# Conversion steps and their additions spread anew over the first slots of a threshold-attention kernel, and pair 0's q turned in two PSUM tiles

## The chip, the cores and the metric

The kernel runs on one core of a Trainium2 chip. The metric is the time of one launch on the device in microseconds (us). Engines are named as the profile names them: PE is TensorE's matmul stream and PEld its weight loads, DVE is VectorE, ACT is ScalarE, POOL is GpSimd, SP is SyncE, which here only issues DMAs. "L208" is line 208 of the kernel as it was before the change.

## The reference

Two blocks follow each other. The first is attention with a threshold, over 8 batches of 8 heads, 576 rows and 64 columns per head:

```python
scores = scale * np.matmul(q, k.transpose(0, 1, 3, 2))
thresh = np.max(scores, axis=-1, keepdims=True) - tau
scores = np.where(scores >= thresh, scores, -1000000000.0)
scores = scores - np.max(scores, axis=-1, keepdims=True)
attn = np.exp(scores)
attn = attn / (np.sum(attn, axis=-1, keepdims=True) + 1e-09)
return np.matmul(attn, v).astype(np.float32)
```

The second takes the result as x, 4608 rows of 512, through two layers with an exact GELU between them:

```python
h = x @ w_in
inv_sqrt2 = np.float32(1.0 / np.sqrt(2.0))
g = 0.5 * h * (1.0 + erf(h * inv_sqrt2))
return (g @ w_out).astype(np.float32)
```

`w_in` is 512 x 2048 and `w_out` 2048 x 512. Both weight arrays reach the kernel as float64, 8 bytes an element, while the kernel computes in float32. It therefore converts them on the chip.

## The kernel before, in words

**Pairs, chunks and slots.** Two heads make a pair; the 64 columns of the two heads fill the 128 partitions. The 576 rows of a pair are four chunks of 128 rows and a tail of 64. The tails of both heads share one chunk (number 4), so a pair has five chunks, and the main loop (L1169 to L1291) runs over slots, each one chunk of one pair. In chunks 0 to 3 a slot has two heads and so two score tiles, two maxima, two exponentials. Chunk 4 has one of each: it is called a one-head slot here. The first batch, four pairs, is ordered apart: slots 0 to 7 are chunks 0 and 1 of pairs 0 to 3, slots 8 to 19 are chunks 2, 3 and 4 of pairs 0 to 3. So slots 10, 13, 16 and 19 have one head. From slot 20 on come the other batches.

**One slot.** `scores` (L432) has PE write the scores of the chunk into PSUM. `softmax_head` has DVE take the negated row maximum (`nmx`, L444), POOL make the threshold from it (`thr`, L447) and ACT the exponential (`p`, L449). `softmax_tail` (L465, DVE) zeroes what lies under the threshold and sums the rows. PE transposes `p` in the next slot (L373), ACT copies the transposes out (L383, L395), and PE multiplies with v (`weigh_v`, L635 and L603). Between these, PE is given matmuls of the second block (`fill`, L703 and others) as soon as there are rows and weights for them.

**The conversion.** The weights are cut in 32 pieces of 128 x 512. SP loads a raw piece (`load_piece`, L184). One step of the conversion is four instructions on three engines: ACT scales the high and the low words (`convert_first`, L200 and L201); DVE shifts and masks the exponent and mantissa (L208) and joins the sign (L209), in `convert_second`, which also loads the next piece; POOL adds the low bits (`add_low_bits`, L220), after which the piece can be used by PE. The list `STEPS` gives the number of steps at the end of each slot. Their additions are not issued with them but wait in a list, `sums_due`, for the next slot's `softmax_head`. There, right after the first maximum has been issued, one addition is put ahead of the threshold on POOL: the newest of the list. After the head, all others follow. The order of every engine's instructions is that in which the program issues them.

**The rest that shares these engines.** `DIVIDE_LATE` tells in which slot the rows of x of a pair are divided by their sums (`divide_late`, L509, two products on POOL). `divisors_early` (L485 to L497) makes those divisors, with DMAs on SP's queue. In slots with `long` set, some of the conversion's ACT work is issued early (`convert_ahead`).

**The start.** `turn_qk_early(0)` turns q and k of pair 0 by matmuls with the identity: `most("k")` turns k in one PSUM tile (L324, copied by DVE at L329), `tails` turns the last 64 rows of both (L336, L341; copies L344, L345, L348), and `most("q", 2)` turns q in two halves of one PSUM tile, each copied by ACT (L327). The tails of q and v are zeroed by DVE (L1128 and L1129), behind four small DVE instructions that need tau (L1118 to L1122).

Of the kernel before, what the change touches and what calls it, by code (L numbers as in the profile page):

```python
# [8 lines left out]
FP32 = mybir.dt.float32  # L9
# [9 lines left out]
def kernel(  # L19
# [28 lines left out]
    nc = tc.nc  # L48
    ctx.enter_context(tc.manual_schedule())

    B, H, S, D = q.shape
    d_model, d_ff = moe_w_in.shape
    P = 128
# [4 lines left out]
    NC = S // P  # L58
# [21 lines left out]
    ps = ctx.enter_context(tc.tile_pool(name="ps", bufs=4, space=PSUM))  # L80
# [21 lines left out]
    def x_slot(want=None):  # L102
        i = max(x_free) if want is None else want
        x_free.remove(i)
        return i
# [8 lines left out]
    def x_rows(i):  # L114
        return xall[:, i, :, :].rearrange("p c t -> p (c t)")
# [5 lines left out]
    ident = const.tile([P, P], FP32, name="ident")  # L121
# [3 lines left out]
    q_tail = [att.tile([P, P], FP32, name=f"q_tail{i}") for i in range(4)]  # L125
    v_sb = [att.tile([P, 2, KR, D], FP32, name=f"v{i}") for i in range(4)]
# [19 lines left out]
    for _ in range(3):  # L146
# [4 lines left out]
    pieces = [(w_in_sb[c][:, f:f + PIECE], moe_w_in[c * P:(c + 1) * P, f:f + PIECE])  # L151
              for f in range(0, d_ff, PIECE) for c in range(N_DM)]
# [60 lines left out]

    sums_due = []

    def add_low_bits(newest=False):

        for _ in range(min(1, len(sums_due)) if newest else len(sums_due)):
            dst, power = sums_due.pop(-1 if newest else 0)
            nc.gpsimd.tensor_tensor(dst, power, dst, op=ALU.add)  # L220
            converted[0] += 1

# [42 lines left out]
    def load_early(p):  # L265
        b, hp = divmod(p, HP)
        s = st[p] = {}
        for name, src in (("q", q), ("k", k)):

            if p == 2:  # L270
                at = s[name + "_slot"] = x_slot()
                t = x_rows(at)[:, 0:2 * (NC + 1) * D].rearrange("p (e c d) -> p e c d", e=2, d=D)
            else:
                t = ld.tile([P, 2, NC + 1, D], FP32, tag=name, name=name)
            s[name] = t
            eng = (nc.scalar, nc.gpsimd)[p] if p < 2 and name == "k" else nc.sync
            for e in range(2):
                rows = src[b, 2 * hp + e, 0:MAIN, :]
                if name == "q":
                    eng.dma_start(t[:, e, 0:NC, :].rearrange("p (g c) d -> p g (c d)", c=2),  # L280
                                  rows.rearrange("(g p c) d -> p g (c d)", p=P, c=2))
                else:
                    eng.dma_start(t[:, e, 0:NC, :], rows.rearrange("(p t) d -> p t d", p=P))
            eng.dma_start(t[0:TAIL, :, NC, :], src[b, 2 * hp:2 * hp + 2, MAIN:S, :].rearrange("e s d -> s e d"))
# [15 lines left out]
    def turn_qk_early(p, names="qk"):  # L300


        s = st[p]
        if names == "k":
            qT, kT = s["qT"], s["kT"]
        elif 2 <= p < HP:
            qT = op.tile([P, MAIN], FP32, tag="o_sb", name="qT")
            kT = pd_tail[p - 2].rearrange("p b i -> p (b i)")
        else:
            qT = ld.tile([P, MAIN], FP32, tag="qT", name="qT")  # L310
            kT = ld.tile([P, TAIL + S], FP32, tag="kT", name="kT")
        s["qT"], s["kT"] = qT, kT
        qt = s["q_tail"] = q_tail[p % 4]
        copy = nc.scalar.copy if p else nc.vector.tensor_copy
        tiles = {name: s.pop(name) for name in names}

        def most(name, parts=1):
            t = tiles[name]
            tr = ps.tile([P, NC, P], FP32, tag="mm", name="tr")
            n = NC // parts  # L320
            for part in range(parts):
                for c in range(part * n, (part + 1) * n):
                    for e in range(2):
                        nc.tensor.matmul(tr[e * D:(e + 1) * D, c, :], lhsT=t[:, e, c, :], rhs=ident, start=True, stop=True)  # L324
                src = tr[:, part * n:(part + 1) * n, :].rearrange("p c s -> p (c s)")
                if name == "q":
                    nc.scalar.activation(qT[:, part * n * P:(part + 1) * n * P], src, AF.Copy, bias=0.0, scale=q_scale)  # L327
                else:
                    copy(kT[:, TAIL:S], src)  # L329

        def tails():
            tr = ps.tile([P, NC, P], FP32, tag="mm", name="tr")
            if "q" in names:
                none = q_tail[HP - 1][0:TAIL, D:2 * D]
                for e in range(2):
                    nc.tensor.matmul(tr[e * D:(e + 1) * D, 0, (1 - e) * TAIL:(2 - e) * TAIL], lhsT=ident[0:TAIL, 0:D],  # L336
                                     rhs=none, start=True, stop=True)
            for j, name in enumerate(names):
                for e in range(2):
                    at = e * TAIL if name == "q" else 0  # L340
                    nc.tensor.matmul(tr[e * D:(e + 1) * D, j, at:at + TAIL], lhsT=tiles[name][0:TAIL, e, NC, :],  # L341
                                     rhs=ident[0:TAIL, 0:TAIL], start=True, stop=True)
            if "k" in names:
                nc.scalar.copy(kT[:, S:S + TAIL], tr[:, j, 0:TAIL])  # L344
                nc.scalar.copy(kT[D:P, 0:TAIL], tr[D:P, j, 0:TAIL])  # L345
            if "q" in names:
                yield
                nc.scalar.activation(qt, tr[:, 0, :], AF.Copy, bias=0.0, scale=q_scale)  # L348

        if p == 0:  # L350
            most("k")
            rest = tails()
            next(rest)
            most("q", 2)
            next(rest, None)
            return
        for name in names:
            most(name)
        for _ in tails():
            pass  # L360
        x_free.extend(s.pop(name + "_slot") for name in names if name + "_slot" in s)
# [73 lines left out]
    def softmax_head(p, i):  # L435

        s = st[p]
        n = len(s["sc", i])
        nmx = small.tile([P, 2], FP32, tag="nmx", name="nmx")
        thr = s["thr", i] = small.tile([P, 2], FP32, tag="thr", name="thr")  # L440
        w = s["p", i] = work.tile([P, 2 * S], FP32, tag="p", name="p")
        for e in range(n):
            sc = s["sc", i][e][:, :, 0:HALF]
            nc.vector.tensor_reduce(nmx[:, e:e + 1], sc, axis=AXIS.XY, op=ALU.max, negate=True)  # L444
            if e == 0:
                add_low_bits(True)
            nc.gpsimd.tensor_scalar(  # L447
                thr[:, e:e + 1], nmx[:, e:e + 1], -1.0, tau_eff, op0=ALU.mult, op1=ALU.subtract)
            nc.scalar.activation(  # L449
                w[:, e * S:(e + 1) * S].rearrange("p (h s) -> p h s", h=2), sc, AF.Exp, bias=nmx[:, e:e + 1], scale=1.0)  # L450
# [23 lines left out]
    def invert(p, i):  # L474

        den = st[p]["sum", i]
        nc.vector.reciprocal(den, den)
# [636 lines left out]
        assert not beside  # L1114

    load_early(0)
    some = const.tile([P, 1], FP32, name="some")
    nc.vector.tensor_scalar(some, tau_sb, 0.0, None, op0=ALU.is_ge)  # L1118
    nc.vector.tensor_scalar(q_scale, some, SCALE, None, op0=ALU.mult)
# [5 lines left out]
    load_early(2)  # L1125
    for _ in range(4):
        load_piece(nc.sync)
    for t in q_tail + [t[:, :, NC, :] for t in v_sb]:  # L1128
        nc.vector.memset(t, 0.0)  # L1129
    turn_qk_early(0)  # L1130
    load_v_early(0)
    load_early(3)
# [23 lines left out]

    PARTS = 1.3, 1.3, 0.2, 1.3, 0.9

    DIVIDE_LATE = {14: 0, 16: 1, 19: 2, 22: 3}
    STEPS = [0, 1, 1, 1, 1, 1, 1, 1, 1, 2, 2, 2, 3, 2, 2, 3, 3, 3, 1, 0, 1]  # L1160
    BUSY = {1: 2, 6: 2, 8: 2}

    tokens = 0
# [5 lines left out]
    for n in range(len(slots) + WEIGH + 1):  # L1169
        p, i = slots[n] if n < len(slots) else divmod(n, SLOTS)  # L1170
        early = p < EARLY
        last = slots[n - 1] if 0 < n <= len(slots) else None
        if p < NP:
            scores(p, i)
            softmax_head(p, i)
            add_low_bits()
            if last and last[0] < EARLY and last[1] < 2:
                invert(*last)
            if last and last[0] < EARLY and last[1] == NC:
                divisors_early(last[0])  # L1180
            if p == 0 and i == 0:
                turn_qk_early(1)
            elif p < HP - 1 and i < 2 and n > 1:
                turn_qk_early(p + 1, "qk"[i])
        elif n == len(slots):
            early_end.close()
            weights_first()
# [16 lines left out]
        if long:  # L1204
            convert_ahead(STEPS[n] - 1)
        if n in DIVIDE_LATE:
            divide_late(DIVIDE_LATE[n])
        if p > EARLY and i == WEIGH:
# [56 lines left out]
        elif n in (BATCH - 2, BATCH - 1):  # L1265
            turn_qk(HP, "k" if n == BATCH - 2 else "q")
        convert(STEPS[n] if n < len(STEPS) else 0)
        if not early:
# [58 lines left out]
```

## Time and profile before

| | us |
|---|---|
| runs | 1329.33, 1327.56, 1326.86 |
| their median | 1327.56 |
| the profiled execution | 1327.03 |
| its span, first to last instruction | 1325.3 |
| PE busy | 1313.4 (99%) |
| DVE busy | 1042.8 (79%) |
| ACT busy | 601.9 (45%) |
| POOL busy | 634.2 (48%) |

The span is part of the profiled execution; the 1.7 us around it belong to the launch. The busy shares are means over the whole span. Up to about slot 20 (120.75 us) all four engines are loaded, after it PE alone is nearly always busy. The first row maxima of the slots concerned are at 53.30 us (slot 9), 58.77 (10), 63.76 (11), 69.23 (12), 76.55 (13), 82.50 (14), 88.46 (15), 95.29 (16), 102.77 (17), 110.58 (18), 116.01 (19) and 120.75 (20).

The durations, in us, that matter for those slots, as the groups and the timeline of the profile have them: L208 0.42 where nothing disturbs it, L209 0.69, L444 0.75, L465 0.82, L447 0.29, L449 0.74, L200 and L201 0.70 each, L220 1.27, L509 0.74 and 0.32. Instructions that follow each other directly on DVE or ACT overlap by some 0.08 us in the records, so a step of L208 and L209 takes 1.07 and the second of two L465 adds 0.74.

### The profile page before, as it was taken

Reading aid. Unit: us, or ns where it says so; the run is one execution under the profiler, and the core shown is the slowest. Engines: PE = TensorE matmul, PEld = TensorE weight load, DVE = VectorE, ACT = ScalarE, POOL = GpSimd, SP = SyncE. Lnnn points to the kernel's source line nnn. Section 1 sums busy time; section 2 is a strip of 40 time slices with the busy share of each in tenths; the row PEclk is TensorE's granted clock in tenths of the full one; section 3 lists DMA queues with packets and bytes.
Section 4 is the critical chain, followed back from the end, with each engine's and each line's share of the span. In section 5 each row is a group of like instructions: output and inputs, shape, how many; then the busy total and the mean of one; then the engine's idle time right before and its main releaser. Section 6 shows DMA issues by size and latency. Waiting matters only on the chain.

```text
span 1325.3 us, 19980 instructions
## 1 busy us (share of the span) xinstructions
PE 1313.4 (99%) x6362; PEld 890.3 (67%) x6362; DVE 1042.8 (79%) x2009; ACT 601.9 (45%) x1018; POOL 634.2 (48%) x1058
## 2 busy tenths in 40 slices
PE   9999999999999999999999999999999999999998
PEld 7775476576476466466466466478778787877877
DVE  6888877888888888888888888883857698386674
ACT  7888266376376367357457438232111203211120
POOL 3565555465555555565555541236364403645430
PEclk9999999999999999999999999999999999999999
DMA  8453676767777777787787775400000140000003
GB/s 256 161 178 106 145 164 159 166 156 168 189 164 164 191 181 165 193 190 168 184 192 170 176 165 115 100 9 0 1 1 0 40 110 11 0 1 0 1 0 80
DMA packets 213688, 153.14 MB, mean 116 GB/s; under 512 B 117264, under 2 KB 196992, under 8 KB 213584
## 3 DMA queue, kind: packets, MB, share of 16 engines
q1 hardware_dynamic: 195440, 125.31, 40.4%
q0 software_dynamic: 17712, 26.26, 7.5%
q8 instruction: 52, 0.85, 0.3%
q14 instruction: 52, 0.43, 0.1%
q10 hardware_dynamic: 432, 0.30, 0.1%
HBM read 56.62 MB, written 12.58 MB: 52 GB/s over the span
## 4 chain that ended last, share of the span: by engine, by line
PE 93%; DVE 2%; issue 1%; DMA 1%; ACT 1%; POOL 1%; SPq 0%; POOLq 0%; DVEq 0%; ACTq 0%
PE bank L891 34%; PE o_ps L718 17%; PE hT L703 16%; PE sc L432 13%; PE xT L603 11%; PE tr L373 1%; DVE nmx L444 1%; PE xT L635 1%; PE tr L324 1%; DVE power L209 1%; DVE power L208 0%; ACT p L449 0%; DVE p L465 0%; DMA inv<-turned 0%; DMA turned_p<-in_moe_w_out_dram 0%
## 5 line engine op out<-in xcount | busy, mean ns | idle before, releaser
L449 ACT ACTIVATE p<-sc,nmx 128x576 f32<-128x576 f32 x288 | 201.9, 737 | 280.0 <-DVE nmx L444 279.8
L465 DVE SCALAR_TENSOR_TENSOR p<-sc,thr,p 128x576 f32<-128x576 f32 x288 | 225.2, 815 | 70.6 <-ACT p L449 62.2
L447 POOL TENSOR_SCALAR thr<-nmx,tau_eff 128x1 f32<-128x1 f32 x288 | 83.9, 293 | 333.3 <-DVE nmx L444 331.2
L703 PE MATMUL hT<-xall,w_in 128*128 128x256 f32 x1024 | 241.8, 385 | 0.0
L444 DVE TENSOR_REDUCE nmx<-sc 128x1 f32<-128x576 f32 x288 | 205.4, 750 | 41.9 <-PE sc L432 40.7
L718 PE MATMUL o_ps<-w_out,g 128*128 128x512 f32 x512 | 236.8, 603 | 0.0
L703 PEld LDWEIGHTS hT<-xall,w_in 128*128 128x128 f32 x1024 | 189.4, 190 | 51.3 <-issue 24.0
L773 DVE TENSOR_TENSOR o<-o,bank 128x256 f32<-128x256 f32 (+1 forms) x242 | 100.1, 417 | 94.5 <-PE bank L891 89.5
L773 DVE TENSOR_TENSOR c<-c,bank 128x320 f32<-128x320 f32 x304 | 147.2, 487 | 33.7 <-PE bank L891 20.1
L718 PEld LDWEIGHTS o_ps<-w_out,g 128*128 128x128 f32 x512 | 93.1, 190 | 109.5 <-issue 107.2
L432 PE MATMUL sc<-kT,qT 64*128 64x288 f32 x960 | 160.1, 429 | 1.5 <-DVE p L465 1.4
L564 DVE STREAM_TRANSPOSE turned_p<-p 128x1152 f32<-128x1152 f32 x112 | 154.4, 1378 | 3.9
L603 PE MATMUL xT<-pT,v 128*64 128x320 f32 (+1 forms) x1200 | 153.6, 410 | 0.0
L432 PEld LDWEIGHTS sc<-kT,qT 64*128 64x128 f32 x960 | 91.2, 186 | 75.9 <-issue 61.1
L603 PEld LDWEIGHTS xT<-pT,v 128*64 128x64 f32 x1200 | 83.4, 137 | 68.0 <-issue 10.4
L891 PE MATMUL bank<-w_out,c 128*128 128x256 f32 (+1 forms) x484 | 120.5, 379 | 0.8 <-DVE o L773 0.8
L261 POOL DMA_DIRECT2D v<-in_v_dram x208 | 110.8, 536 | 3.6 <-issue 1.4
L891 PEld LDWEIGHTS bank<-w_out,c 128*128 128x128 f32 x484 | 90.3, 190 | 19.0 <-DVE o L773 3.2
L958 ACT ACTIVATE c<-c 128x320 f32<-128x320 f32 (+1 forms) x80 | 46.8, 623 | 114.7 <-DVE c L773 114.7
L773 POOL TENSOR_TENSOR c<-c,g 128x320 f32<-128x320 f32 (+1 forms) x40 | 50.5, 1271 | 67.5 <-DVE c L773 67.5
L891 PE MATMUL bank<-t_out,g 128*128 128x256 f32 (+1 forms) x324 | 82.4, 377 | 0.4 <-DVE o L773 0.4
L891 PE MATMUL bank<-t_out,c 128*128 128x256 f32 x320 | 82.7, 381 | 0.0
(188 smaller groups left out, 1755.9 us busy)
## 6 DMA issues: line engine op xcount, KB each, us to landing
pT<-turned_p SPq DMA_DIRECT2D x448, 160.0 KB, 3.5
pT<-pd_tail SPq DMA_DIRECT2D x112, 80.0 KB, 3.0
q<-in_q_dram POOLq DMA_DIRECT2D x104, 72.0 KB, 3.7
k<-in_k_dram POOLq DMA_DIRECT2D x104, 72.0 KB, 3.2
inv<-turned SPq DMA_DIRECT2D x54, 128.0 KB, 4.1
v<-in_v_dram POOLq DMA_DIRECT2D x156, 40.0 KB, 3.1
out_dram<-o SPq DMA_DIRECT2D x40, 128.0 KB, 2.4
xall<-in_moe_w_out_dram SPq DMA_DIRECT2D x9, 512.0 KB, 4.8
```

The lines of the kernel that those rows point to most:

```text
L261: eng.dma_start(t[r:P:4, e, 0:n, :], rows[:, r * KR:r * KR + n, :])
L432: nc.tensor.matmul(sc[e][:, h, 0:HALF], lhsT=lhsT, rhs=s["kT"][rows, at:at + HALF], start=True, stop=True)
L444: nc.vector.tensor_reduce(nmx[:, e:e + 1], sc, axis=AXIS.XY, op=ALU.max, negate=True)
L447: nc.gpsimd.tensor_scalar(thr[:, e:e + 1], nmx[:, e:e + 1], -1.0, tau_eff, op0=ALU.mult, op1=ALU.subtract)
L449: nc.scalar.activation(w[:, e * S:(e + 1) * S].rearrange("p (h s) -> p h s", h=2), sc, AF.Exp, bias=nmx[:, e:e + 1], scale=1.0)
L465: nc.vector.scalar_tensor_tensor(row, sc[e][:, :, 0:HALF], thr[:, e:e + 1], row, op0=ALU.is_ge, op1=ALU.mult, accum_out=den[e])
L564: nc.vector.transpose(turned_p[:, :, i // 2, 0:NB, i % 2 * Q:(i % 2 + 1) * Q], w.rearrange("p (e b i) -> p e b i", e=2, i=Q))
L603: nc.tensor.matmul(to, lhsT=s["v"][:, e, c, :], rhs=rhs, start=(c == 0), stop=(c == KR - 1))
L703: nc.tensor.matmul(hT[:, j % 2, :], lhsT=w_in_sb[c][:, j * P:(j + 1) * P], rhs=x_blk[n][:, c, :], start=(c == 0), stop=(c == N_DM - 1))
L718: nc.tensor.matmul(o[:, 0:d_model], lhsT=g[j][:, m * P:(m + 1) * P], rhs=w_out_sb[j], start=(j == 0), stop=(j == N_DF - 1))
L773: eng.tensor_tensor(out, a, b, op=ALU.add)
L891: nc.tensor.matmul(to, lhsT=l, rhs=r, start=start and k == 0, stop=k == len(pairs) - 1, skip_group_check=not start)
```

## The change

Five things change.

- In `most` each part of pair 0's q gets a PSUM tile of its own.
- The memsets of the tails of q and v are issued ahead of the four DVE instructions that need tau.
- `add_low_bits` takes a number, and always the oldest additions. In the head it issues one; after the head it issues at most one in the one-head slots of the first four pairs, and all elsewhere.
- `STEPS`: slots 10, 13 and 16 go from 2, 2, 3 to 1 each; slots 11, 14, 18, 19 go from 2, 2, 1, 0 to 3, 3, 2, 1. The total stays at 32.
- `DIVIDE_LATE`: pair 1 is divided in slot 17 and no longer in slot 16.

```diff
-    def add_low_bits(newest=False):
+    def add_low_bits(most):
 
-        for _ in range(min(1, len(sums_due)) if newest else len(sums_due)):
-            dst, power = sums_due.pop(-1 if newest else 0)
+        for _ in range(min(most, len(sums_due))):
+            dst, power = sums_due.pop(0)
             nc.gpsimd.tensor_tensor(dst, power, dst, op=ALU.add)
             converted[0] += 1
...
         def most(name, parts=1):
             t = tiles[name]
-            tr = ps.tile([P, NC, P], FP32, tag="mm", name="tr")
             n = NC // parts
             for part in range(parts):
-                for c in range(part * n, (part + 1) * n):
+                tr = ps.tile([P, n, P], FP32, tag="mm", name="tr")
+                for c in range(n):
                     for e in range(2):
-                        nc.tensor.matmul(tr[e * D:(e + 1) * D, c, :], lhsT=t[:, e, c, :], rhs=ident, start=True, stop=True)
-                src = tr[:, part * n:(part + 1) * n, :].rearrange("p c s -> p (c s)")
+                        nc.tensor.matmul(tr[e * D:(e + 1) * D, c, :], lhsT=t[:, e, part * n + c, :], rhs=ident,
+                                         start=True, stop=True)
+                src = tr.rearrange("p c s -> p (c s)")
...
             if e == 0:
-                add_low_bits(True)
+                add_low_bits(1)
...
     load_early(0)
+    for t in q_tail + [t[:, :, NC, :] for t in v_sb]:
+        nc.vector.memset(t, 0.0)
     some = const.tile([P, 1], FP32, name="some")
...
-    for t in q_tail + [t[:, :, NC, :] for t in v_sb]:
-        nc.vector.memset(t, 0.0)
     turn_qk_early(0)
...
-    DIVIDE_LATE = {14: 0, 16: 1, 19: 2, 22: 3}
-    STEPS = [0, 1, 1, 1, 1, 1, 1, 1, 1, 2, 2, 2, 3, 2, 2, 3, 3, 3, 1, 0, 1]
+    DIVIDE_LATE = {14: 0, 17: 1, 19: 2, 22: 3}
+    STEPS = [0, 1, 1, 1, 1, 1, 1, 1, 1, 2, 1, 3, 3, 1, 3, 3, 1, 3, 2, 1, 1]
...
             scores(p, i)
             softmax_head(p, i)
-            add_low_bits()
+            add_low_bits(1 if early and i == NC else len(pieces))
```

## The prediction

> **What bounds the kernel now.** I looked first at the table of windows (length, then busy us and instructions of PE, PEld, DVE, ACT, POOL, then clock, DMA share, GB/s).
>
> ```profile
> 60.00:70.00 10.00, 9.52 (x55) 6.53 (x55) 9.22 (x20) 9.04 (x19) 5.68 (x9) 1.00 0.46 157
> 80.00:90.00 10.00, 9.28 (x54) 5.84 (x53) 9.49 (x18) 9.10 (x20) 6.39 (x11) 1.00 0.77 284
> 100.00:110.00 10.00, 8.18 (x47) 5.46 (x47) 9.76 (x19) 9.37 (x19) 5.62 (x9) 1.00 0.49 187
> 130.00:160.00 30.00, 29.97 (x96) 13.48 (x96) 24.95 (x45) 9.57 (x15) 15.18 (x31) 1.00 0.70 149
> 160.00:1325.00 1165.00, 1159.14 (x5330) 784.92 (x5326) 912.20 (x1737) 483.51 (x786) 552.08 (x914) 1.00 0.47 108
> ```
>
> From 130 us on PE never rests, and its order is the same in both programs, so what is gained or lost up to slot 20 (120.75 us) reaches the end one for one. Before that DVE is fuller than PE wherever PE stops. The chain of waits at the start, then PE's worst stop in the timeline:
>
> ```profile
> 6.96 0.61 PE tr L324 x8
> 7.57 0.02 issue
> 7.59 0.48 ACT qT L327
> 8.07 0.04 issue
> 8.12 0.66 PE tr L324 x8
> 8.78 1.22 PE sc L432 x8
> ```
>
> ```profile
> 105.57 1.94 PE L432 MATMUL sc<-pd_tail,qT 64*128 64x288 f32 x8 [1.81 <-DVE p L465]
> ```
>
> PE waits for ACT to copy half of pair 0's q before it turns the other half. Later its stops (0.47 at 66.55, 0.71 at 85.29, 1.81 here) wait for L465: DVE's order, which the change rewrites. The DVE and POOL timelines of slot 16:
>
> ```profile
> 97.95 1.51 DVE L208 TENSOR_SCALAR power<-power 128x512 uint32<-128x512 uint32 x1
> 99.49 1.11 DVE L209 SCALAR_TENSOR_TENSOR power<-xall,power 128x512 uint32<-128x512 uint32 x1
> 100.53 0.54 DVE L208 TENSOR_SCALAR power<-power 128x512 uint32<-128x512 uint32 x1
> ```
>
> ```profile
> 96.67 2.50 POOL L220 TENSOR_TENSOR w_out<-power,w_out 128x512 uint32<-128x512 uint32 x2
> 99.13 1.65 POOL L509 TENSOR_TENSOR xall<-xall,w_out 128x256 f32<-128x256 f32 x2
> ```
>
> L208 takes 0.42 undisturbed, but 1.51 here: it ends 0.29 after the addition (99.46 against 99.17). At 61.31, 79.32 and 106.07 (0.74, 1.21, 1.74 us) it again ends about 0.28 after a POOL instruction. L209 (0.69 undisturbed) takes 1.11 while L509 runs. So the two engines take turns.
>
> [...] L444 and L465, which read PSUM, keep 0.75 and 0.82 beside running additions. [...]
>
> **The change, part by part.**
>
> Two PSUM tiles. The second eight L324 no longer wait for ACT: their 0.57 us stop goes. The first scores still need the first copy (done 8.06) and the second turns, which would then end near 8.1. Scores 8.71 to 8.11: **-0.6**. The second copy follows at 8.06, hidden behind scores (1.2 us).
>
> Memsets. Eight of 0.15 us move into the 3.57 us in which DVE waits for tau (4.80). L336 could start sooner, but L341 at 6.45 waits for q's tail, landed 6.40: **0**. Without this cover the price is 1.2 us, on DVE's kT copy at 6.52.
>
> Conversions. 23 steps fall into slots 9 to 19 either way, so L200, L201, L208, L209, L220 and the piece loads cost nothing by number. On DVE's path a two-head slot lasts A + 2x0.74 + 1.07k + B + R: A is first L444 to first L465; 2x0.74 the two L465; 1.07 a step, L208 and L209; k steps; B the time blocked; R what else is waited for. A one-head slot has 0.74 once.
>
> A: 1.80 if the head's addition and threshold end last (addition starts 0.15 after the last L209, 1.27, threshold 0.29), 1.63 if exp does. Popping the newest made the addition wait for the slot's last L209. Popping the oldest lets it start after the FIRST L209 of a group. POOL then [...] should win ahead of the second L209, which it holds for about 0.95 (1.27 less the 0.32 that passes before L209 would start). So A falls 0.17 and B rises 0.95 in each group of two or more. Second, where three steps follow three, two additions remain after the head and run into the first L208: 1.04 each, like 79.32's 0.79 and 97.95's 1.09. Before, such blocks stood in slots 13, 16, 17.
>
> I carried starts forward by this rule for every instruction of both programs: traced duration, latest of engine and operands[...]. For before it gives each slot's start within 0.03 us up to 17, and 0.27 too early by 20. Slot lengths, first L444 to the next slot's:
>
> | slot | k before/after | B before/after | length before/after |
> |---|---|---|---|
> | 9 | 2/2 | 0.19/1.14 | 5.46/6.42 |
> | 10 | 2/1 | 0.31/0.08 | 4.98/3.52 |
> | 11 | 2/3 | 0/0.25 | 5.47/7.76 |
> | 12 | 3/3 | 0/1.99 | 7.30/8.29 |
> | 13 | 2/1 | 0.77/0.09 | 5.95/3.93 |
> | 14 | 2/3 | 0.55/1.46 | 5.96/8.37 |
> | 15 | 3/3 | 0/1.99 | 6.82/8.29 |
> | 16 | 3/1 | 1.65/0.08 | 7.50/3.52 |
> | 17 | 3/3 | 1.09/0.46 | 7.56/8.59 |
> | 18 | 1/2 | 0.37/1.26 | 5.42/7.23 |
> | 19 | 0/1 | 0/0 | 4.73/4.64 |
>
> Sums 67.15 and 70.56: +3.41. By term: B 4.93 to 8.80, **+3.87**; A 20.03 to 18.80, **-1.23**; R 4.27 to 5.04, **+0.77**. R grows because three steps outrun ACT: its L200 for the second stands behind copies that wait for PE's turns, 1.0 us in slot 11 and 1.7 in 17, less what slots 12, 15 and 19 no longer wait.
>
> Cap of one addition after the head: without it one-head slots carry a second, but their one step meets it little; within 0.2 either way, taken 0.1 gain, in the table. DIVIDE_LATE: L509 (0.74 + 0.32) and SP's loads queued past it move one slot; it blocks L208 by 0.45 in slot 17 (table), 0 to 1 if it falls otherwise. SP: in slots 10, 13, 16 a piece load stands behind divisor DMAs, L489 to L497, and v's loads; those pieces still land over 5 us before ACT takes them: 0; if not, L200 is late and a step with it. PE's idle rises by what DVE loses.
>
> Sum: -0.61 + 3.41 + 0.05 (slots 21 to 24) = **+2.85**. The carried before is 0.27 short, which may be an order effect that the change removes, so +2.6 to +2.85; I take +2.7. Against the profiled execution (1327.03, span 1325.3) that is 1329.7, span 1328.0; against the median of the runs, 1327.56, which lies 0.5 above it, **1330.3**.
>
> **The rivals.**
>
> 1. L209 keeps its place[...]. For it: only about 0.2 us separate the claims, and POOL's spans are rough. Against it: at 856.56 a DVE instruction was held for 0.65 beyond its 0.82 by a POOL one begun 0.07 earlier. Carried forward without L209's blocks: +0.3. **1327.9**, same.
>
> 2. Other side: the start keeps its 0.6, and blocks move rather than grow. The mechanism is slots 12 and 15: two additions after the head, 2.5 us, start 0.17 sooner because the oldest pops early, and if thresholds let them finish before L465 they block nothing: 2 x 1.04 saved. With rival 1's price of +0.3 that is -1.8: **1325.8**. It decides once additions end 0.9 us sooner than carried. Against: at 79.32 and 97.95 they did not.
>
> 3. R larger: POOL's late additions hold up L703 on PE (0.5 already in PE's weight-load waits), or ACT is a step later in slots 12, 14 and 15 as in 11 and 17: 1.0 to 1.7 more. **1331.8**, slower.
>
> That the change does nothing is excluded: the order on DVE, ACT and POOL differs.
>
> **How the numbers follow.** About 0.2% (2.65 us) is what a measurement of this kernel can tell from no change: 1324.9 to 1330.2. Forecast 0.50, rival 1 0.22, rival 2 0.08, rival 3 0.20. The forecast lies on the limit: with 1 us either way on its stalls, 0.29 slower and 0.21 same. Rival 1 is 0.21 same, 0.01 slower; rival 2 0.05 faster, 0.03 same; rival 3 slower. Sum: slower 0.50; same 0.45; faster 0.05. Range 1326.3 to 1332.4: it leaves out rival 2's better part and rival 3's worst. For forecast and rival 3 alone, 1329.0 to 1332.4.
>
> **What would show it.** Scores first at 8.1, no 0.57 wait at L324. In groups of steps from slot 9 (near 57.6), L209 of about 1.6, once per group of two or more, with L220 beside it; L208 near 1.4 in slots 12, 14 and 15; L444 to L465 1.63 in slots 10, 12, 15, 18. PE's waits for DVE before L432 up by about 3 in slots 12 to 18. If L209 stays at 0.69, rival 1 holds. If PE's late stage (from 130 us) changes by more than 1 us, the one-for-one carry is wrong.

## The result

The changed kernel is slower: 1332.15 us, median of 14 runs, against 1328.41 for the kernel before, median of 14 beside it. The ratio is 1.0021, with a 95% interval of 1.0011 to 1.0031: 2.8 us more, between 1.5 and 4.1 (the two medians themselves lie 3.7 apart). The forecast was 1330.3, 2.7 us over the median it started from. Single runs scatter by 4.4 us in the kernel before and by 6.1 in the changed one; the last section of this document has one reason. Of the runs of the experiments, one of 2706.97 us (without the cap) and one of 1504.57 us (the version that beats both) stand apart from all others and are left out.

The profiled execution took 1332.42 us, span 1330.7, 5.4 us more than before. Its page has the same share for PE (99%), and PE still sets the end. The lines of the changed kernel named here are numbered one higher than in the text of the prediction, but for L200 to L220 and L324, which keep their numbers: L445 is the maximum, L466 the masking, L448 the threshold, L433 the scores, L374 the transposes of p. The windows of the first 160 us (columns as in the prediction) show where PE rests:

```profile
70.00:80.00 10.00, 8.54 (x45) 6.82 (x42) 9.59 (x15) 8.23 (x18) 4.39 (x5) 1.00 0.67 153
80.00:90.00 10.00, 9.80 (x61) 6.67 (x61) 7.91 (x16) 8.66 (x18) 7.82 (x11) 1.00 0.74 270
90.00:100.00 10.00, 9.54 (x53) 7.48 (x49) 9.65 (x16) 7.70 (x16) 4.39 (x5) 1.00 0.57 169
100.00:110.00 10.00, 8.50 (x38) 6.26 (x40) 6.74 (x15) 6.90 (x15) 8.04 (x11) 0.83 0.60 221
130.00:160.00 30.00, 29.97 (x88) 13.76 (x89) 24.31 (x45) 12.79 (x21) 15.06 (x31) 1.00 0.66 139
```

From 130 us on PE is as full as before. In the first 130 us it idles more, and in one window its granted clock is 0.83: that is new. DVE's timeline of slot 9 and POOL's beside it:

```profile
56.93 0.69 DVE L209 SCALAR_TENSOR_TENSOR power<-xall,power 128x512 uint32<-128x512 uint32 x1
57.54 0.43 DVE L208 TENSOR_SCALAR power<-power 128x512 uint32<-128x512 uint32 x1
58.01 1.65 DVE L209 SCALAR_TENSOR_TENSOR power<-turned_p,power 128x512 uint32<-128x512 uint32 x1
59.58 0.74 DVE L445 TENSOR_REDUCE nmx<-sc 128x1 f32<-128x576 f32 x1
```

```profile
57.70 1.40 POOL L220 TENSOR_TENSOR w_in<-power,w_in 128x512 uint32<-128x512 uint32 x1 [1.09 <-DVE power L209]
```

The addition becomes free when the first L209 is done (57.62), and its record begins at 57.70, while the second L208 runs (to 57.97); it is 1.40 long for 1.27 and ends at 59.10. The second L209, begun at 58.01, ends 0.56 after it and takes 1.65 for 0.69. The next slot's maximum stands behind it. The same line has 1.64 or 1.65 in slots 12, 15 and 18. Slot 12 has both kinds of block, the two additions left over after the head and the early one:

```profile
74.00 1.47 DVE L208 TENSOR_SCALAR power<-power 128x512 uint32<-128x512 uint32 x1
75.50 0.69 DVE L209 SCALAR_TENSOR_TENSOR power<-xall,power 128x512 uint32<-128x512 uint32 x1
76.11 0.42 DVE L208 TENSOR_SCALAR power<-power 128x512 uint32<-128x512 uint32 x1
76.57 1.64 DVE L209 SCALAR_TENSOR_TENSOR power<-turned_p,power 128x512 uint32<-128x512 uint32 x1
```

```profile
72.65 2.53 POOL L220 TENSOR_TENSOR w_in<-power,w_in 128x512 uint32<-128x512 uint32 x2
76.34 1.32 POOL L220 TENSOR_TENSOR w_in<-power,w_in 128x512 uint32<-128x512 uint32 x1 [1.16 <-ACT g L671]
```

For the last of these the profile names an ACT copy, which ended at 76.22; the L209 that the addition needs ended at 76.19.

Slot lengths (first maximum to the next slot's), from the two timelines, beside what was forecast for after:

| slot | before | after, forecast | after | B after |
|---|---|---|---|---|
| 9 | 5.47 | 6.42 | 6.41 | 1.17 |
| 10 | 4.99 | 3.52 | 3.43 | 0.01 |
| 11 | 5.47 | 7.76 | 7.88 | 0.28 |
| 12 | 7.31 | 8.29 | 8.30 | 2.01 |
| 13 | 5.95 | 3.93 | 3.80 | 0.01 |
| 14 | 5.96 | 8.37 | 8.16 | 0.97 |
| 15 | 6.83 | 8.29 | 8.30 | 2.01 |
| 16 | 7.48 | 3.52 | 3.58 | 0.01 |
| 17 | 7.81 | 8.59 | 10.23 | 0.47 |
| 18 | 5.43 | 7.23 | 7.23 | 1.29 |
| 19 | 4.73 | 4.64 | 4.54 | 0.01 |
| sum | 67.43 | 70.56 | 71.86 | 8.24 |

Ten of the eleven lie within 0.21 us of the forecast. Slot 17 is 1.64 longer. PE's windows around it:

```profile
103.00:104.00 1.00, 1.00 (x3) 0.69 (x3) 0.97 (x2) 0.90 (x3) 1.00 (x1) 0.50 0.92 377
105.00:106.00 1.00, 1.00 (x4) 0.73 (x4) 1.00 (x3) 0.22 (x1) 1.00 (x1) 0.50 0.94 374
107.00:108.00 1.00, 1.00 (x7) 0.83 (x6) 0.74 (x2) 0.00 (x0) 0.56 (x3) 1.00 0.00 0
```

For about 3.4 us PE's granted clock was 0.50, a half clock for short. What that costs can be read from fourteen matmuls of slot 17, of the kernel before and then of the changed one:

```profile
99.93 3.29 PE L703 MATMUL hT<-xall,w_in 128*128 128x256 f32 x14
```

```profile
103.22 4.83 PE L704 MATMUL hT<-xall,w_in 128*128 128x256 f32 x14
```

They take 1.54 us more. ACT's copies of PE's transposes come later by it, so does the L200 behind them, and DVE stands still for it for 3.25 us in slot 17, where the forecast has 1.7. The stop of PE ahead of the half clock is a new one, in PE's and ACT's timelines of slot 16:

```profile
98.81 1.04 PE L374 MATMUL tr<-ident,p 128*128 128x128 f32 x8
101.50 0.33 PE L374 MATMUL tr<-ident,p 128*128 128x128 f32 x1 [1.66 <-ACT g L671]
```

```profile
100.23 0.74 ACT L450 ACTIVATE p<-sc,nmx 128x576 f32<-128x576 f32 x1 [1.95 <-DVE nmx L445]
100.87 0.58 ACT L671 COPY g<-hT 128x512 f32<-128x512 f32 x1
```

DVE's maximum is late (the blocked L209 stands ahead of it), so ACT's exponential is late, so the copy of g behind it on ACT is late, and PE waits for the PSUM tile that this copy frees. This is where the loss enters PE in slots 12, 13, 16 and 18: PE's waits for L374 behind the copy sum to 4.3 us, while its waits before the scores fell from 3.4 to 1.0.

Scores of slot 22 come 4.44 us later than before, of which the half clock is about 1.5. The other 1.0 us of the span arises after 560 us (1.5 by 615 us, of it 0.34 in a wait of PE for a DMA, and 0.5 back by 690); it is within what two executions differ by there, as told below.

### The profile page after: what moved, and what is told of

It reads as the page before. It is cut to its first block, busy times and chain, and to the rows that moved or that the text cites. A ratio compares the mean times of both kernels' runs of the same rounds, so it can differ in the third digit from the quotient of the medians.

```text
span 1330.7 us, 19981 instructions
## 1 busy us (share of the span) xinstructions
PE 1316.2 (99%) x6362; PEld 892.1 (67%) x6362; DVE 1045.3 (79%) x2009; ACT 602.1 (45%) x1018; POOL 636.9 (48%) x1058
## 4 chain that ended last, share of the span: by engine, by line
PE 94%; DVE 3%; ACT 1%; issue 1%; DMA 0%; POOL 0%; SPq 0%; DVEq 0%; POOLq 0%; ACTq 0%
PE bank L892 34%; PE o_ps L719 17%; PE hT L704 16%; PE sc L433 14%; PE xT L604 11%; PE tr L374 1%; DVE power L208 1%; DVE nmx L445 1%; ACT p L450 1%; DVE power L209 1%; PE xT L636 1%; PE tr L324 1%; DVE p L466 0%; DMA turned<-turned 0%; PE idle L147 0%
## 5 line engine op out<-in xcount | busy, mean ns | idle before, releaser
L466 DVE SCALAR_TENSOR_TENSOR p<-sc,thr,p 128x576 f32<-128x576 f32 x288 | 225.2, 815 | 69.5 <-ACT p L450 63.9
L448 POOL TENSOR_SCALAR thr<-nmx,tau_eff 128x1 f32<-128x1 f32 x288 | 84.7, 295 | 349.0 <-DVE nmx L445 347.7
L445 DVE TENSOR_REDUCE nmx<-sc 128x1 f32<-128x576 f32 x288 | 205.2, 749 | 40.9 <-PE sc L433 39.7
L433 PE MATMUL sc<-kT,qT 64*128 64x288 f32 x960 | 159.9, 429 | 1.6 <-DVE p L466 1.3
L433 PEld LDWEIGHTS sc<-kT,qT 64*128 64x128 f32 x960 | 91.3, 186 | 75.7 <-issue 60.7
```

Source lines behind the costliest of these rows:

```text
L433: nc.tensor.matmul(sc[e][:, h, 0:HALF], lhsT=lhsT, rhs=s["kT"][rows, at:at + HALF], start=True, stop=True)
L448: nc.gpsimd.tensor_scalar(thr[:, e:e + 1], nmx[:, e:e + 1], -1.0, tau_eff, op0=ALU.mult, op1=ALU.subtract)
L466: nc.vector.scalar_tensor_tensor(row, sc[e][:, :, 0:HALF], thr[:, e:e + 1], row, op0=ALU.is_ge, op1=ALU.mult, accum_out=den[e])
```

## The experiments

Four theories were to be told apart: DVE's L209, held up by additions that the new order lets start early; the new places of the steps, by ACT's late conversions; the cap and the division; and PE's granted clock. Times are ratios to the kernel before, run beside, with 95% intervals. "Slot 22" is the start of its first scores in the profile, against 132.45 before and 136.89 after.

**The start alone.** The two PSUM tiles and the memsets stay, all else is as before.

```diff
-            dst, power = sums_due.pop(0)
+            dst, power = sums_due.pop(-1 if most == 1 else 0)
...
-    STEPS = [0, 1, 1, 1, 1, 1, 1, 1, 1, 2, 1, 3, 3, 1, 3, 3, 1, 3, 2, 1, 1]
+    STEPS = [0, 1, 1, 1, 1, 1, 1, 1, 1, 2, 2, 2, 3, 2, 2, 3, 3, 3, 1, 0, 1]
...
-            add_low_bits(1 if early and i == NC else len(pieces))
+            add_low_bits(len(pieces))
```

> Only the two PSUM tiles for pair 0's q and the memsets moved ahead; conversions, additions and divisions as before. Theory (the start is worth its 0.57 us stop, carried to the end): no stop at the second turning of q, first scores at most 2.1 us after the q_tail turns (before 2.62), slot lengths 9 to 19 as before within 0.05 us, time about 0.6 us under before (1327.8 against 1328.4). Rival (the gain is eaten by the landing of pair 0's loads, which the profile after showed 0.4 us later): scores start no earlier than 8.6 and the time is that of before within 0.2 us.

Measured: 1.0002 (0.9991 to 1.0013). The division is in slot 16 again too. The second turning of q no longer stops, and slots 9 to 17 are as before within 0.03 us; slots 18 and 19 are 0.8 and 0.6 longer, in and behind a half clock that the profile of the kernel before does not have. The expected gain does not show in the times. In this profile the tail of q came late:

```profile
7.07 0.33 PE L342 MATMUL tr<-ident,q 64*64 64x64 f32 x4 [1.39 <-DMA q<-in_q_dram]
7.45 1.09 PE L324 MATMUL tr<-ident,q 128*64 128x128 f32 x16
8.68 1.00 PE L433 MATMUL sc<-kT,qT 64*128 64x288 f32 x6
```

Both theories hold in part: the stop is gone, and the landing decides what is seen of it. Over the nine profiles with the new start the first scores come at 7.76 to 8.68 us, mean 8.21; the two with the old start have 8.71 and 8.75. Counted from the first turn of q, so without the landing, they come after 1.23 or 1.24 us in all nine and after 1.82 in both others: the gain is 0.59 us, too little for the times to show.

**The newest addition again.** The changed kernel, with its new steps, but `add_low_bits` in the old order.

```diff
-            dst, power = sums_due.pop(0)
+            dst, power = sums_due.pop(-1 if most == 1 else 0)
...
-            add_low_bits(1 if early and i == NC else len(pieces))
+            add_low_bits(len(pieces))
```

> The changed kernel, but the head pops the newest addition again and all others follow the head, in every slot: the new STEPS, DIVIDE_LATE, start and memsets stay. Theory (the loss is the oldest addition [...]): no L209 over 0.8 in slots 9 to 19 except beside divisions, first L444 to first L465 back at 1.80 in slots 10, 12, 15 and 18; carried forward, scores of slot 22 are 0.4 us before those of before, time about 0.3 under before (1328.1), that is about 3 us under the changed kernel. Rival (the steps' new places cost, by ACT's late L200 and three steps in a row): time stays at about 1331, 2.5 us over before.

Measured: 0.9991 (0.9985 to 0.9998), 1326.76 us; slot 22 at 131.74, 0.7 sooner than in the kernel before. In slot 9 (DVE, then POOL):

```profile
57.00 0.43 DVE L208 TENSOR_SCALAR power<-power 128x512 uint32<-128x512 uint32 x1
57.46 0.69 DVE L209 SCALAR_TENSOR_TENSOR power<-turned_p,power 128x512 uint32<-128x512 uint32 x1
58.07 0.75 DVE L445 TENSOR_REDUCE nmx<-sc 128x1 f32<-128x576 f32 x1
```

```profile
58.30 1.27 POOL L220 TENSOR_TENSOR w_in<-power,w_in 128x512 uint32<-128x512 uint32 x1 [2.25 <-DVE power L209]
```

The addition begins after the group, and L209 takes 0.69. With the steps in their new places and only the order of additions and the cap put back, the loss is gone (the cap alone makes no difference that the times show, see below): the steps do not cost. Nor do they gain: from the first scores to those of slot 22 it takes 123.73 us here and 123.74 before, so the 0.7 us are the start's. One expectation missed. Slots 13 and 16 have an L209 of 1.65, where no division runs: after a group of three, the two additions behind the head reach the single step of a one-head slot, and here they catch L209. This is the late kind of block, at a place that was not foreseen.

**The old steps with the new order of additions.**

```diff
-    DIVIDE_LATE = {14: 0, 17: 1, 19: 2, 22: 3}
-    STEPS = [0, 1, 1, 1, 1, 1, 1, 1, 1, 2, 1, 3, 3, 1, 3, 3, 1, 3, 2, 1, 1]
+    DIVIDE_LATE = {14: 0, 16: 1, 19: 2, 22: 3}
+    STEPS = [0, 1, 1, 1, 1, 1, 1, 1, 1, 2, 2, 2, 3, 2, 2, 3, 3, 3, 1, 0, 1]
```

> The changed kernel with STEPS and DIVIDE_LATE of before: the oldest-first additions and the cap stay, the steps go back. Theory (oldest-first costs 0.95 in each group of two or more steps, of which the old list has nine, slots 9 to 17): eight or nine L209 of about 1.65, scores of slot 22 about 5.8 us later than before, time about 1334. Rival (the new STEPS cost): time at or under that of before, 1327.8 to 1328.4, since the steps are as before and the start gains.

Measured: 1.0035 (1.0022 to 1.0047), slot 22 at 138.69, 6.2 later than before. L209 takes 1.64 to 1.66 eight times in slots 9 to 17. The groups by shape, from 10 to 130 us, of this kernel and then of the changed one (busy, mean ns):

```profile
L209 DVE SCALAR_TENSOR_TENSOR power<-turned_p,power 128x512 uint32<-128x512 uint32 x15 | 15.6, 1039 | 0.5
L209 DVE SCALAR_TENSOR_TENSOR power<-xall,power 128x512 uint32<-128x512 uint32 x16 | 14.4, 898 | 0.5
```

```profile
L209 DVE SCALAR_TENSOR_TENSOR power<-turned_p,power 128x512 uint32<-128x512 uint32 x15 | 13.3, 883 | 0.5
L209 DVE SCALAR_TENSOR_TENSOR power<-xall,power 128x512 uint32<-128x512 uint32 x16 | 12.0, 753 | 0.5
```

Before, the same two groups had 692 and 717 ns. B over slots 9 to 19 sums to 12.96 us here, where before has 5.26 and the changed kernel 8.24. So by the profiles the order of additions alone loses more than the whole change, and the new steps, with fewer groups of two or more, give part of it back; by the times the two kernels are not told apart (the intervals overlap), and some of the 6.2 us is a half clock of 6.8 us.

**Short additions, new order and old order.** In both kernels L220 covers 32 of 512 columns, which takes 0.25 us where nothing disturbs it.

```diff
-            nc.gpsimd.tensor_tensor(dst, power, dst, op=ALU.add)
+            nc.gpsimd.tensor_tensor(dst[:, 0:32], power[:, 0:32], dst[:, 0:32], op=ALU.add)
```

> The changed kernel with each addition (L220) over 32 of its 512 columns only, so that it lasts about 0.3 us in place of 1.27; the low bits of the other columns are left out of the weights. Order, waits and DMAs are those of the changed kernel. Theory [...]: no L209 over 0.75 and no L208 over 0.75 except beside divisions, L444 to L465 at most 1.66 in two-head slots, scores of slot 22 about 2 us before those of before, time about 1326.4, some 5 us under the changed kernel. Rival (ACT's conversions and the order of steps set the slots, the additions only fill the waits): slots 11, 12, 14, 15 and 17 still 7.7 to 8.6 us, time within 1.5 us of the changed kernel's 1332.1.

> The kernel before, with each addition (L220) over 32 of its 512 columns only; the low bits of the other columns are left out of the weights. It is the counterpart of the fourth experiment: what short additions are worth to the old order. Theory (the old order already hides most of the additions, since the newest waits until the last L209 is done; blocks of L208 in slots 13, 17 and 18 and part of 16 go, 3 of 4.9 us, of which PE takes up part): scores of slot 22 about 1.1 us before those of before, time 1326.9 where before stands at 1328.0; so the fourth experiment's gain over the changed kernel, 5 us and more, is mostly the price of the new order of additions. Rival (short additions are worth the same 4 to 5 us to any order): slot 22's scores 3 us or more sooner, time under 1325.

Measured: the new order 0.9978 (0.9968 to 0.9988), slot 22 at 129.52; the old order 0.9988 (0.9981 to 0.9994), slot 22 at 130.98. Slot 9 of the new order (DVE, then POOL):

```profile
56.90 0.43 DVE L208 TENSOR_SCALAR power<-power 128x512 uint32<-128x512 uint32 x1
57.37 0.69 DVE L209 SCALAR_TENSOR_TENSOR power<-turned_p,power 128x512 uint32<-128x512 uint32 x1
```

```profile
57.06 0.38 POOL L220 TENSOR_TENSOR w_in<-power,w_in 128x32 uint32<-128x32 uint32 x1 [1.09 <-DVE power L209]
```

The addition comes as early as in the changed kernel, but ends 0.07 us after L209's record begins, and L209 keeps its 0.69. Shorter additions give the new order 0.0043 (5.7 us: from 1.0021 to 0.9978) and the old one 0.0012 (1.6 us). With them the new order is no longer the slower one: slot 22 comes 1.46 us sooner than in the old order, 0.83 of it by the start, though the intervals of the times overlap. Of the rival, this much holds: slots 11 and 17 keep 7.66 and 8.44 us, where DVE waits 1.10 and 1.91 us for ACT's L200, while 12 and 15 fall to 6.73 and 6.30. Slot 22 came 2.9 us sooner than before, for 2 expected, in the new order, and 1.5 for 1.1 in the old one.

**Without the cap; the division back in slot 16.**

```diff
-            add_low_bits(1 if early and i == NC else len(pieces))
+            add_low_bits(len(pieces))
```

```diff
-    DIVIDE_LATE = {14: 0, 17: 1, 19: 2, 22: 3}
+    DIVIDE_LATE = {14: 0, 16: 1, 19: 2, 22: 3}
```

> The changed kernel with all additions issued after the head in every slot: the cap of one in the one-head slots is gone, all else as changed. Theory (one step in those slots meets a second addition only slightly): first maxima of slots 11, 14, 17 and 20 within 0.4 us of the changed kernel's but for a change of granted clock, time 1332 within 0.6 us. Rival (the cap, by pushing additions into slots 12 and 15, makes their 1.04 blocks of L208): those blocks fall under 0.3 and the time falls by about 2 us.

> The changed kernel with pair 1's division back in slot 16. Theory (moving it is neutral: its 1.06 us of POOL fits beside slot 16's one step as beside slot 17's three): slot lengths as in the changed kernel within 0.2 us, B of slot 17 down by 0.3 to 0.5 but slot 17 no shorter since ACT's second L200 is awaited there; time within 0.5 us of the changed kernel. Rival (the division in slot 17 is what makes slot 17 long): slot 17 at least 0.5 us shorter and the time with it.

Measured: 1.0024 (1.0011 to 1.0036) and 1.0024 (1.0016 to 1.0032), neither apart from the changed kernel's 1.0021. Without the cap the blocks of 1.03 stay in slots 12 and 15, and slots 13 and 16 get one more each (0.80 and 0.96). This profile has no half clock, and its slots 9 to 19 sum to 70.83. One expectation missed: slot 17's first maximum comes 1.3 us later after slot 9's than in the changed kernel, not 0.4 at most. Slot 17 gives it back (7.91, where the changed kernel has 10.23), since DVE waits 1.05 us for ACT's L200 there and not 3.25. With the division in slot 16, that slot is 0.5 longer, B of slot 17 falls from 0.47 to 0.11, and slot 17 takes 9.74, 0.5 less, with a half clock in it again: more than the 0.2 us expected for either slot, but the two cancel. Both edits are neutral within 2 us, which is what these intervals can tell.

**PE's stop filled.** The kernel of the first experiment, with idle matmuls ahead of slot 17's scores, where PE has slack. They push PE's next work back by 1.7 us, once the earlier start of this execution is allowed for. So its stop, which lies ahead of the scores of slot 18 (the expectation says 17), closes without a change in DVE's order.

```diff
-    BUSY = {1: 2, 6: 2, 8: 2}
+    BUSY = {1: 2, 6: 2, 8: 2, 16: 3}
```

> The kernel of the first experiment (steps, additions and divisions as before, new start) with three pairs of idle matmuls with the identity put on PE at the end of slot 16, ahead of the scores of slot 17, where PE stands still for 1.8 us until DVE frees the score tile. Theory (a PE stop of over about 1.6 us is followed by a lower granted clock, seen at 0.5 to 0.7 after such stops in three profiles): no 5 us window from 90 to 130 us with a granted clock under 1.0, DVE's slots unchanged, time 0.5 to 1.3 us under the first experiment's 1328.85. Rival (the clock falls by itself, whatever PE does there): the dip near 105 to 115 us stays and the time is that of the first experiment within 0.4 us.

Measured: 0.9997 (0.9989 to 1.0005), 1327.09 us. The first line is the stop in the first experiment, in PE's timeline. Below it are the windows of 105 to 110 us of that kernel and, third, of this one:

```profile
105.59 2.44 PE L433 MATMUL sc<-pd_tail,qT 64*128 64x288 f32 x8 [1.82 <-DVE p L466]
```

```profile
105.00:110.00 5.00, 4.39 (x16) 2.12 (x18) 4.90 (x10) 4.94 (x12) 2.55 (x3) 0.69 0.13 28
```

```profile
105.00:110.00 5.00, 4.89 (x30) 2.53 (x30) 4.90 (x8) 4.94 (x11) 2.07 (x3) 1.00 0.14 28
```

In the same 5 us PE gets 30 matmul records done in place of 16, none of them idle ones (those run from 98.47 to 100.07). DVE's slots 9 to 17 are the same to 0.02 us in both; slots 18 and 19 are 5.44 and 4.73 here, 6.19 and 5.30 there. From the first scores to those of slot 22 it takes 123.77 us here, 125.12 there and 123.74 in the kernel before: a half clock costs 1.35 us at this place. The mean granted clock was at or under 0.998 in 2 of 14 runs here, and in 8 of 13 of the first experiment. The times alone don't part the two, and one profile without a half clock proves little, since the kernel before has none in its profile either, with the stop; the count of the runs speaks for the theory.

**A version that beats both.** New start, old order of additions, pair 1 divided in slot 17, and, against the list of the kernel before, one step each taken from slots 13 and 16. The edit of the additions is that of the second experiment; the edit of the steps, against the changed kernel:

```diff
-    STEPS = [0, 1, 1, 1, 1, 1, 1, 1, 1, 2, 1, 3, 3, 1, 3, 3, 1, 3, 2, 1, 1]
+    STEPS = [0, 1, 1, 1, 1, 1, 1, 1, 1, 2, 2, 2, 3, 1, 2, 3, 2, 3, 2, 1, 1]
```

> A version for both goals: new start, division of pair 1 in slot 17, newest addition in the head and all others after it, and STEPS of before with one step moved from slot 13 to 14 ... 2, 2, 2, 3, 1, 2, 3, 2, 3, 2, 1, 1 for slots 9 to 20: slots 13 and 16 give one step each to slots 18 and 19. Theory (each blocked L208 or L209 is paid in full, so steps should leave the slots that follow a group of three, where two or three additions run late): B summed over slots 9 to 19 at most 4.0, scores of slot 22 about 2.4 us before those of before, time about 1326.0 (2.2 under before). Rival (only the start and the granted clock matter): time that of the second experiment, 1326.8, or of before.

Measured: 0.9985 (0.9976 to 0.9994), 1325.8 us; slot 22 at 130.19, 2.3 sooner than before, 0.3 of it by the start. B over slots 9 to 19 sums to 3.84, where before has 5.26 and after 8.24. This is the fastest kernel of the study that does the whole computation, though its interval overlaps the one of the newest addition again.

## Why the prediction was right

**Two PSUM tiles, -0.6.** Right in mechanism and size: no stop at the second turning, and 0.59 us from the first turn of q to the scores. What was not in it is that the landing of q and k moves the first scores by 0.9 us from run to run.

**Memsets, 0.** Not contradicted: in the profiles with the new start the turning of the tails waits for the landing of q or k, never for a memset. No run has the memsets alone.

**B, +3.87.** Measured 5.26 to 8.24, +2.98. The four blocked L209 and the L208 of slots 12 and 15 stand where they were put, with 0.96 and 1.04. That an addition gets ahead of the second L209 was an estimate of the forecast: in the profile of the kernel before, the longest L209, beside a division, is 1.11 us. Over-counted: slot 14, 0.97 for 1.46, where no L209 takes more than 0.69, and several blocks of 0.08 that don't exist. The sentence that B rises by 0.95 in each group of two or more is too wide: seven groups are that long, and four have a blocked L209. In the other three (slots 11, 14 and 17) DVE stands still ahead of the second L208, for 1.02, 0.78 and 3.25 us, until ACT's L200 is done, and the addition runs in that pause; what is left of it holds the L208 (0.70 and 0.93 in slots 11 and 14) and not the L209. Also before was under-counted by 0.33, mostly in slot 17 (1.33 for 1.09).

**A, -1.23.** Measured 20.08 to 18.62, -1.46; 1.62 or 1.63 in slots 10, 12, 15 and 18.

**R, +0.77.** What is left of the slots' +4.43 is +2.91. The wait for ACT's L200 in slot 11 is 1.02 us, as forecast (1.0); in slot 17 it is 3.25 for 1.7, and the half clock's 1.54 explains the excess. The granted clock is a term that the prediction lacked. Without it R is about +1.4 and the slots' sum about +2.9, where the forecast has +3.41: B was too high by 0.9, R too low by some 0.6, and A not low enough by 0.2. The profile without the cap, which has no half clock, comes to +3.40, but by other parts: slots 13 and 16 are 1.5 us longer than the forecast has them with the cap, slots 14 and 17 are 1.2 shorter.

**The amount: in part luck.** The start's -0.6 and the slots' +2.9 make +2.3. The runs give 2.8, with an interval of 1.5 to 4.1, so that they can't tell 2.3 from the forecast's 2.7, and agreement to 0.1 is chance. The half clock can hardly be part of that difference: it is no rarer before (mean clock at or under 0.998 in 33 of 77 runs beside the first eight experiments) than after (5 of 14); the two profiles differ by it, since only the changed kernel's has one. The median of 1332.15 lies nearer to the third rival's 1331.8 than to the forecast's 1330.3, because the kernel before, measured beside it, stands at 1328.41, 0.85 above the base of the forecast.

**Cap, division, SP's loads, 0.1 to 0.5 at most.** Nothing against them in the experiments.

**One for one to the end.** Right as far as can be told. Between slot 22 and the end of the span the changed kernel needs 1193.8 us, the one before 1192.8. Of the eleven profiles, ten lie between 1192.4 and 1193.8, and two kernels that differ by idle matmuls alone (the first experiment and PE's stop filled) are 1.0 apart; the eleventh (the better version, 1196.0) has a half clock at 683 us.

**Where PE would wait: wrong.** Its waits before the scores did not rise by 3, they fell. The step that failed is "PE's waits for DVE before L432 up by about 3": the scores were taken as the only place where PE depends on DVE, while L374 depends on it too, by way of ACT's queue. The amount was not touched by this, since DVE's slots were what was summed.

**The rivals.** The first (L209 keeps its place) fell by L209's 1.65. The second (blocks move and vanish) fell by L208's 1.47 in slots 12 and 15. The third expected 1.0 to 1.7 more, by late weights or by ACT being a step later in slots 12, 14 and 15. Those slots kept to the forecast or were shorter (8.30, 8.16 and 8.30 for 8.29, 8.37 and 8.29). Some 1.5 us did come in the profile by late ACT, in slot 17, but from the clock, which the rival did not name.

## What to carry to other kernels

Here DVE and POOL took turns: an addition on POOL that was freed in the middle of a group on DVE got in between the group's instructions, and most of its length (0.96 of 1.27 us) was paid by what stood behind them. Where traces show two engines to hold each other up like this, let the operation of the second depend on the last instruction of the group, as the old order did (L209 at 0.69 in slot 9), even where an older operand would let it start sooner. And read where a delay on DVE enters PE from the queues between them: here it came through the engine that copies PSUM, not through the scores.

## What the runs showed of the hardware

**The half clock after short stops.** PE's granted clock fell after stops of 1.66 (changed kernel), 1.82 (first experiment), 2.32 (old steps), 1.64 (division back) and, at 681 us, 1.40 us (the better version). It did not after 1.81 (before), 1.64 and 1.45 (no cap) or 1.46 us (changed kernel, slot 12). Windows of 1 us have it at 0.50 in the changed kernel (above) and, first and second here, with the old steps and in the better version:

```profile
111.00:112.00 1.00, 1.00 (x4) 0.33 (x1) 0.97 (x2) 1.00 (x3) 1.00 (x1) 0.50 0.24 56
```

```profile
684.00:685.00 1.00, 1.00 (x4) 0.81 (x3) 0.98 (x3) 0.98 (x2) 0.19 (x1) 0.50 0.95 246
```

In the changed kernel it lasted 3.41 us (102.95 to 106.36), in the better version 3.4 and with the old steps 6.8. The windows of 5 us of the other two (0.69 and 0.97 in the first experiment, 0.66 with the division back) are what 3.4 us at 0.50 would give.

The length of a stop alone does not tell. The first experiment and the kernel before have the same stop, 1.82 and 1.81 us, and only the first has a half clock in its profile; 1.64 us was followed by one with the division back and not without the cap. What else decides was not shown.

The mean clock was at or under 0.998 in 33 of 77 runs of the kernel before that lay beside the first eight experiments, in 2 of 14 where its stop was filled, and in none of 21 of the newest addition again, whose longest stop ahead of 128 us is 1.1 us. So part of what that version gains is clock. It is also one reason why single runs scatter: the 33 runs of the kernel before have a median of 1329.0 us and the other 44 one of 1327.2; of the changed kernel's 14 runs, the five at or under 0.998 have 1332.6 and the other nine 1330.6.

**The addition that waits goes first.** Between an L208 and the L209 behind it the records leave 0.03 to 0.04 us, and yet an addition whose record began during that L208 was paid for by the L209, which took 1.64 to 1.66 us for 0.69: four times in the changed kernel, eight with the old steps. In slots 9, 12, 15 and 18 of the changed kernel the additions' records begin 0.27, 0.19, 0.19 and 0.19 us before the end of the L208, and the L209 take 1.65, 1.64, 1.65 and 1.65. The short addition at such a place in slot 9, 0.38 us long, left the L209 at 0.69.
